# Reading raw blocks of w2's inner operands straight from the weights, and k of some chunks in one transfer

## The chip, the cores and the metric

The kernel runs on one core of a Trainium2 chip. The core has five engines that run their own queues of instructions in order: TensorE (PE: matmuls, with PEld for loading weights), VectorE (DVE), ScalarE (ACT), GpSimd (POOL) and SyncE (SP), which here issues nearly all DMA transfers. The metric is the time of one execution on the device in microseconds (us), given as the median of several runs.

## The reference

Two blocks follow each other, all in fp32. First a causal linear attention with a decay per head, over 4 batches, 8 heads, 768 positions and head size 64; then a mixture of 4 experts over the 3072 tokens (512 wide), with hidden size 1024 and 512 outputs, weighted by normalized probabilities:

```python
# attention, per block of 64 positions
intra = (qb @ kb^T * Dmask) @ vb
inter = (qb * lam_pow) @ kv_state
out   = intra + inter
kb_dec   = kb * rev_pow
kv_state = lam_block * kv_state + kb_dec^T @ vb
...
# experts, on x = the attention's output, 3072 x 512
p = domain_probs / (domain_probs.sum(-1, keepdims=True) + 1e-09)
for e in range(E):                       # E = 4
    h = np.maximum(x @ w1[e], 0.0)       # w1[e] is 512 x 1024
    out += p[:, e:e + 1] * (h @ w2[e])   # w2[e] is 1024 x 512
```

## The kernel before, in words

**Tiling.** The tokens are cut into 24 chunks of 128 and 3 groups of 8 chunks. A *unit* is one group with one expert, 12 in all, in the order (0,0) (0,1) (0,2) (0,3) (1,1) (1,2) (1,3) (1,0) (2,2) (2,3) (2,0) (2,1). Each unit has a first product (x with w1, lines 1125 to 1165) and a second one (hidden with w2). Both use Strassen-Winograd's scheme: seven products M1 to M7 of blocks, where one operand is a block of the weights (A11, A12, A22) or a sum of blocks (S1 to S4), and the other is a block or a sum of blocks (T1 to T4) of the data. The operands are: M1 uses A11, M2 A12, M3 S4, M4 A22, M5 S1, M6 S2, M7 S3. In what follows, M1, M2 and M4 are *A-type* products and M3, M5, M6 and M7 are *S-type* products.

**The nested second product.** From unit 5 on (`NEST`), each of the seven products of the second product is itself done by the scheme: in order M1, M3, M5, M7, M6, M2, M4 (`SEQ3`), each with seven inner products in the order M1, M7, M6, M4, M5, M2, M3 (`INNER`). For that, each product's weight operand is cut in four and its inner sums S1 to S4 are needed as well: seven inner operands (A11, S3, S2, A22, S1, A12, S4), each of 128 x 2 x 128 numbers, 128 KB. They are made once for each expert, stored in device memory as `w2_ops[expert, product]`, and read back for each unit.

**Making them.** `prepare_w2_ops` (line 335) gives a list of *chores*: load blocks of w2 (`block`, tile w2b, 256 KB per transfer), add or subtract them on POOL (`total`, tile w2o), and, by `ready`, call `inner_w2` (line 322), which makes the four inner sums of one product on POOL (tile ops, four operations of 128 x 256) and queues their storing. Of one product, all seven operands are stored, also those which are plain blocks of w2. The chores of the four experts are appended in the order 2, 3, 0 (before unit 0) and 1 (at unit 5). Those of experts 3, 0 and 1 are *eased*: they use another pool of tiles and end with M6, M2, then the total S4 and M3. Expert 0 is used first in unit 7, expert 1 in unit 11, which is the last (`FINAL`); there M2 is done without nesting (`PLAIN`), straight from the weights.

**Reading them.** `feed3` (line 1249) loads the operands of one product for PE into four tiles w2t (two operands each; six such tiles are there in turn). It is called some tiles ahead of their use. In unit 11 all products but the first are read as one whole tile (w2s). Line 1514 holds the inner matmuls that use the tiles, line 1207 the second products that are not nested, line 1148 the first products. `tt` (line 117) is the helper through which all additions on VectorE and POOL go, `send` (line 114) the one for nearly all transfers.

**What sets the order.** The program writes out all instructions in one pass, with a clock `now` that counts steps of PE's work. After each step `pump` (line 202) may begin the next chore. It does so only if the counts of the planner allow it: `asked` (0.27 for each transfer sent through `send`) and `moved` (by the bytes of a transfer and the length of its contiguous pieces) must be less than `FULL` = 4 ahead of `now`, and the last chore's spacing, 5 or 7 steps in the nested part, must be over. Stores wait in a queue until 8 steps after POOL's counted work. Where an operand is needed that has not been made and stored, `until` (line 226) begins chores and stores, all that is needed, without regard to these counts:

```python
def until(what):
    while what not in made:
        pump(force=True)
```

The engines then run what was written, each in its own order, as soon as what it waits for is there. Transfers on SP's queue are issued in order, so one that waits for its data holds up all behind it.

**Attention.** The 24 chunks go through a pipeline beside the products of the experts. `load` (line 155) fetches q, k and v of a chunk, `decayed` (line 657) multiplies k with the decay on POOL. The chunks from 13 on *come across* (`comes_across`, line 481): their q and k are also copied to device memory in another layout and turned on VectorE instead of PE. Their k in natural layout is still needed for the state, and is fetched by two transfers, one for each half of the heads, straight through SP and not through `send`.

Of the kernel before, what the change touches and what calls it, by code (L numbers as in the profile page):

```python
# [12 lines left out]
ALU = mybir.AluOpType  # L13
# [8 lines left out]
def kernel(  # L22
# [30 lines left out]
    nc = tc.nc  # L53

    B, H, S, D = q.shape
# [3 lines left out]
    C = P  # L59
# [32 lines left out]
    def small(name):  # L92
        return pool.tile([P, W], FP32, name=name, tag="t")
# [66 lines left out]
    def load(n, names="qkv"):  # L160

        c, b = where(n)
        for name in names:
            x = ({"k": acc_tile, "v": w2_tile} if n < CPG else {}).get(name, small)(f"{name}n")
            src = {"q": q, "k": k, "v": v}[name][b, :, c * C:(c + 1) * C, :]
            if name == "v":
                to, of = x[:].rearrange("p (h d) -> p h d", d=D), src.rearrange("h p d -> p h d")
                for h in (slice(0, 4), slice(4, 8)) if n < CPG else (slice(0, 8),):
                    send(out=to[:, h], in_=of[:, h], by=nc.scalar if n == 0 and h.start else None)
            else:  # L170
                to, of = x[:].rearrange("p (i r d) -> p i r d", r=2, d=D), src.rearrange("(r i) p d -> p i r d", r=2)
                for r in range(2):
                    by = nc.scalar if n == 0 and r == 1 else nc.sync
                    by.dma_start(out=to[:, :, r], in_=of[:, :, r])  # L174
            nat[n, name] = x[:].rearrange("p (h d) -> p h d", d=D)


# [15 lines left out]
    def store(f):  # L193
        queue.append((busy[0] + (8 if spare else 2), f))
# [31 lines left out]
# [3 lines that stand above are left out]
# [91 lines left out]


    INNER = ("M1", "M7", "M6", "M4", "M5", "M2", "M3")

    def inner_w2(e, m, blk, two):
        b = {f"A{i + 1}{j + 1}": blk[j][:, :, i * P:(i + 1) * P] for i in range(2) for j in range(2)}
        s = [x.rearrange("p c d -> p (c d)").rearrange("p (k c d) -> p k c d", k=2, c=2) for x in two("ops")]
        for name, x, y, op in S_OPS:
            b[name] = s[SLOT[name] // 2][:, SLOT[name] % 2]
            tt(nc.gpsimd, b[name], b[x], b[y], op)
        to = w2_ops[e, MS.index(m)]  # L330
        b["S3"] = s[0]
        at = (("A11", 0), ("S3", slice(1, 3)), ("A22", 3), ("S1", 4), ("A12", 5), ("S4", 6))
        store(lambda: ([send(out=to[:, x], in_=b[n]) for n, x in at], made.add(("w2", e, m))))

    def prepare_w2_ops(e, eased):
        st = {}

        def two(name):
            if eased:
                t = [small(name)[:] for _ in range(2)]  # L340
            else:
                t = stage.tile([P, 2, W], FP32, name=name, tag="st")
                t = [t[:, q] for q in range(2)]
            return [x.rearrange("p (c d) -> p c d", c=2) for x in t]

        def block(name, i, j):
            t = st[name] = two("w2b")
            for q in range(2):
                r = j * W + q * 256
                src = moe_w2[e, r:r + 256, i * DH:(i + 1) * DH]  # L350
                send(out=t[q], in_=src.rearrange("(c p) d -> p c d", p=P))

        def total(name, a, b, op):
            t = two("w2o")
            for q in range(2):
                tt(nc.gpsimd, t[q], st[a][q], st[b][q], op)
            st[name] = t

        def ready(m):
            inner_w2(e, m, st[A_OF[m]], two)  # L360

        if not eased:
            return weight_steps(block, total, ready)

        def less():
            a, b = st["A11"], st.pop("A21")
            for q in range(2):
                tt(nc.gpsimd, b[q], a[q], b[q], ALU.subtract)
            st["S3"] = b

        def drop(*names):
            for n in names:
                del st[n]

        return [
            lambda: (block("A21", 1, 0), block("A22", 1, 1)), pause(6),
            lambda: total("S1", "A21", "A22", ALU.add),
            lambda: (ready("M4"), block("A11", 0, 0), drop("A22")), pause(4),
            less, lambda: ready("M7"), lambda: (ready("M1"), drop("S3")), lambda: ready("M5"),
            lambda: (total("S2", "S1", "A11", ALU.subtract), block("A12", 0, 1)), lambda: ready("M6"),  # L380
            lambda: ready("M2"),
            lambda: total("S4", "A12", "S2", ALU.subtract), lambda: ready("M3"),
        ]

# [96 lines left out]
    def comes_across(n):  # L481
        return n >= FIRST_ACROSS
# [174 lines left out]
    def decayed(n):  # L657

        kn = nat[n, "k"]
        kd = kn if n >= CPG else small("kd")[:].rearrange("p (h d) -> p h d", d=D)  # L660
        nat[n, "kd"] = kd
        by = k_decay.rearrange("p r ac -> p ac r").unsqueeze(3).to_broadcast([P, NHP, 2, D])
        tt(nc.gpsimd, *(x.rearrange("p (ac r) d -> p ac r d", r=2) for x in (kd, kn)), by, ALU.mult)

    carried = set()

# [20 lines left out]
    def turn(n, tags):  # L687
        all_added()
        begin_state(n)
        if comes_across(n):  # L690
            turn_across(n)
            return
        if n < CPG:
            decayed(n)
        qn, kn = nat.pop((n, "q")), nat[n, "k"]
        qp = bank(tags[0], "qp")
        kp = bank(tags[1], "kp")
        for x, y in ((qp, qn), (kp, kn)):
            for ac in range(NHP):
                nc.tensor.transpose(  # L700
                    out=x[:, ac * C:(ac + 1) * C], in_=y[:, 2 * ac:2 * ac + 2].rearrange("p r d -> p (r d)"),
                    identity=ident[:],
                )
        if n >= CPG:
            decayed(n)
        del nat[n, "k"]
        qT, kT = small("qT"), small("kT")
        nc.scalar.copy(out=qT[:], in_=qp[:])
        nc.scalar.copy(out=kT[:], in_=kp[:])
        if n >= CPG:  # L710
            turned[n] = qT, kT, qT
            return
        qs = small("qs")
        scaled = lambda: scale_q(qs, qp)
        soon(n, scaled)
        turned[n] = qT, kT, qs, scaled

    def scores(n, tags):
# [19 lines left out]
        for ac in range(NHP):  # L738
            for x in range(1 if last else 2):
                for r in range(2):  # L740
                    nc.tensor.matmul(  # L741
                        out=sp[x][half[r], 256 + ac * D:256 + (ac + 1) * D], lhsT=kd[half[x], 2 * ac + r],
                        rhs=vn[half[x], 4 * r + ac], start=False, stop=True, skip_group_check=True,
                    )
        st = small("st")
# [503 lines left out]
    def feed3(e, m, k):  # L1249

        x_e = units[e][1]
        until(("w2", x_e, m))
        if e == FINAL and m != SEQ3[0]:

            if k == 0:
                t = xp.tile([P, 7, 256], FP32, name="w2s", tag="x" + SEQ[SEQ3.index(m)])
                if (e, m) == PLAIN:
                    i, j = int(A_OF[m][1]) - 1, int(A_OF[m][2]) - 1
                    src = moe_w2[x_e, j * W:(j + 1) * W, i * DH:(i + 1) * DH]
                    send(out=t[:, 0:4], in_=src.rearrange("(k p) d -> p k d", p=P))  # L1260
                    fed3[e, m, 0] = t
                    return
                send(out=t[:], in_=w2_ops[x_e, MS.index(m)].rearrange("p k c d -> p k (c d)"))
                for x in range(4):
                    fed3[e, m, x] = t[:, 2 * x:min(2 * x + 2, 7)]
            return
        t = w2pool.tile([P, 2, DH], FP32, name="w2t", tag="w2")
        n = min(2, 7 - 2 * k)
        send(
            out=t[:, 0:n], in_=w2_ops[x_e, MS.index(m), :, 2 * k:2 * k + n].rearrange("p k c d -> p k (c d)"),  # L1270
        )
        fed3[e, m, k] = t

# [218 lines left out]
    def nested_product(e, m, tags):  # L1494
# [8 lines left out]

        def inner(x, i):
            if (e, m) == END and i in ("M2", "M3"):
                turned_product(("M2", "M3").index(i), b[B_OF[i]], fed3[e, m, x // 2][:, x % 2])
                return
            t = tags[0] if i in ("M1", "M6", "M5", "M3") else tags[1]
            fresh = i in ("M1", "M7", "M2")
# [2 lines left out]
            p = banks[t]  # L1512
            for c in range(2):
                nc.tensor.matmul(  # L1514
                    out=p[:, 0:256], lhsT=fed3[e, m, x // 2][:, x % 2, c * P:(c + 1) * P],
                    rhs=b[B_OF[i]][:, c * 256:(c + 1) * 256], start=(fresh and c == 0), stop=True,
                    skip_group_check=True,
                )
# [443 lines left out]
```

## Time and profile before

| what | value |
| --- | --- |
| time, median of 3 runs | 1143.09 us (1141.39 to 1143.7) |
| time of the profiled execution | 1141.95 us |
| span from the first to the last instruction, profiled execution | 1140.2 us |
| mean granted clock of TensorE | 1.000 |
| read / written in device memory | 197.19 MB / 78.68 MB |
| transfers w2t<-w_ops of 256 KB | 129, 3.3 us from issue to landing (median) |
| transfers w2t<-w_ops of 128 KB | 43, 2.2 us |
| transfers w_ops<-ops of 256 KB / 128 KB | 28 / 56, 4.1 / 3.7 us |
| transfers w_ops<-w2b, w_ops<-w2o of 128 KB | 45 and 39, 3.9 us each |
| transfers w2b<-in_moe_w_dram of 256 KB | 56, 4.9 us |
| transfers kn<-in_k_dram of 128 KB | 47, 4.5 us |

The profile names engines PE, PEld, DVE, ACT, POOL and SP; SPq and PEq are the sequencers in front of them. L114 is line 114 of the program. A group is written as operation, tile written <- tiles read, and its count; both `w1_ops` and `w2_ops` appear as w_ops. In rows in order of time, the first number is the start, the second the duration in us from there to the end of what was merged into the row, "x6" the number of instructions, and the brackets at the end hold how long the engine stood idle before, and for what. A waiting line reads: who waited <- for whom: us in total, times, longest.

### The profile page before, as it was taken

Reading aid. Unit: us, or ns where it says so; the run is one execution under the profiler, and the core shown is the slowest. Engines: PE = TensorE matmul, PEld = TensorE weight load, DVE = VectorE, ACT = ScalarE, POOL = GpSimd, SP = SyncE. Lnnn points to the kernel's source line nnn. Section 1 sums busy time; section 2 is a strip of 40 time slices with the busy share of each in tenths; the row PEclk is TensorE's granted clock in tenths of the full one; section 3 lists DMA queues with packets and bytes.
Section 4 is the critical chain, followed back from the end, with each engine's and each line's share of the span. In section 5 each row is a group of like instructions: output and inputs, shape, how many; then the busy total and the mean of one; then the engine's idle time right before and its main releaser. Section 6 shows DMA issues by size and latency. Waiting matters only on the chain.

```text
span 1140.2 us, 22167 instructions
## 1 busy us (share of the span) xinstructions
PE 1130.8 (99%) x7991; PEld 987.7 (87%) x7991; DVE 771.7 (68%) x1472; ACT 381.1 (33%) x770; POOL 767.7 (67%) x734
## 2 busy tenths in 40 slices
PE   8999999999999999999999999999999999999998
PEld 7788888888888888888888888888888888888887
DVE  4576775588577757837655566878767576776785
ACT  4325123212312321232343442444354452342332
POOL 2747148655852984854884997995995873873885
PEclk9999999999999999999999999999999999999999
DMA  8796889899989999987867669976779757657553
GB/s 195 173 281 183 214 226 265 276 299 279 310 270 323 301 311 303 312 279 233 260 204 249 200 182 286 347 241 199 223 235 277 217 161 213 189 159 214 168 194 74
DMA packets 321436, 271.58 MB, mean 238 GB/s; under 512 B 150640, under 2 KB 256304, under 8 KB 321328
## 3 DMA queue, kind: packets, MB, share of 16 engines
q1 hardware_dynamic: 298528, 264.37, 76.1%
q10 hardware_dynamic: 22768, 5.80, 2.5%
q8 instruction: 64, 1.05, 0.4%
q14 instruction: 44, 0.36, 0.1%
q0 software_dynamic: 32, 0.00, 0.0%
HBM read 197.19 MB, written 78.68 MB: 242 GB/s over the span
## 4 chain that ended last, share of the span: by engine, by line
PE 97%; SPq 1%; DMA 1%; DVE 0%; issue 0%; ACT 0%; DVEq 0%
PE pg L1148 41%; PE pq L1514 25%; PE q L1207 21%; PE pM L1656 2%; PE pc L1656 2%; PE op L797 1%; PE sp L734 1%; PE op L815 1%; PE sp L741 1%; DMA qn<-in_q_dram 1%; SPq L114 1%; PE pM L1381 1%; PE pg L1514 1%; SPq L174 0%; PE qp L700 0%; PE kp L700 0%
## 5 line engine op out<-in xcount | busy, mean ns | idle before, releaser
L1148 PE MATMUL pg<-xs,ws_in 128*128 128x256 f32 x1960 | 470.2, 380 | 0.4 <-DVE m L117 0.4
L1148 PEld LDWEIGHTS pg<-xs,ws_in 128*128 128x128 f32 x1960 | 371.0, 190 | 53.5 <-DVE m L117 3.2
L117 DVE TENSOR_TENSOR m<-pg,m 128x512 f32<-128x512 f32 x374 | 255.4, 686 | 91.7 <-PE pg L1148 81.4
L1207 PE MATMUL q<-w2t,m 128*128 128x256 f32 x1120 | 265.6, 380 | 0.0
L1207 PEld LDWEIGHTS q<-w2t,m 128*128 128x128 f32 x1120 | 211.7, 190 | 29.3 <-issue 0.3
L117 DVE TENSOR_TENSOR sums<-pq,sums 128x256 f32<-128x256 f32 x272 | 113.1, 421 | 90.6 <-PE pq L1514 78.4
L117 POOL TENSOR_TENSOR m<-m,decay 128x512 f32<-128x512 f32 x91 | 114.5, 1271 | 82.4 <-ACT m L1165 65.4
L1514 PE MATMUL pq<-acc,w2t 128*128 128x256 f32 x688 | 169.2, 379 | 0.0
L1514 PEld LDWEIGHTS pq<-acc,w2t 128*128 128x128 f32 x688 | 130.5, 190 | 18.0
L1165 ACT ACTIVATE m<-m 128x512 f32<-128x512 f32 x99 | 62.4, 630 | 190.9 <-DVE m L117 186.7
L1225 DVE SCALAR_TENSOR_TENSOR acc<-q,gate,acc 128x256 f32<-128x256 f32 x108 | 52.0, 482 | 75.6 <-PE q L1207 74.8
L117 DVE TENSOR_TENSOR m<-m,m 128x512 f32<-128x512 f32 x108 | 96.6, 894 | 6.5 <-ACT m L1131 6.5
L1161 ACT COPY m<-pg 128x512 f32<-128x512 f32 x88 | 51.5, 586 | 121.6 <-PE pg L1148 114.2
L117 POOL TENSOR_TENSOR acc<-hT,hT 128x512 f32<-128x512 f32 x56 | 70.3, 1270 | 21.7 <-PE pq L1514 13.9
L1125 ACT COPY pg<-m 128x512 f32<-128x512 f32 x77 | 45.5, 591 | 110.2 <-DVE m L117 108.1
L117 POOL TENSOR_TENSOR acc<-hT,acc 128x512 f32<-128x512 f32 x56 | 71.2, 1272 | 7.0 <-PE pq L1514 3.2
L1514 PE MATMUL pq<-hT,w2t 128*128 128x256 f32 x288 | 70.0, 379 | 0.0
L117 POOL TENSOR_TENSOR w2o<-w2b 128x512 f32<-128x512 f32 x26 | 36.7, 1437 | 45.6 <-DMA w2b<-in_moe_w_dram 39.3
L1514 PEld LDWEIGHTS pq<-hT,w2t 128*128 128x128 f32 x288 | 54.7, 190 | 7.4
L117 POOL TENSOR_TENSOR kn<-kn,decay 128x512 f32<-128x512 f32 x16 | 19.1, 1197 | 55.9 <-PE kp L700 29.8
L1129 ACT COPY m<-pg 128x512 f32<-128x512 f32 x44 | 25.7, 585 | 91.8 <-PE pg L1148 91.8
L1514 PE MATMUL pq<-m,w2t 128*128 128x256 f32 x228 | 55.4, 379 | 0.0
(157 smaller groups left out, 1453.3 us busy)
## 6 DMA issues: line engine op xcount, KB each, us to landing
w2t<-w_ops SPq DMA_DIRECT2D x129, 256.0 KB, 3.3
ws_in<-w_ops SPq DMA_DIRECT2D x40, 512.0 KB, 4.7
ws_in<-w_ops SPq DMA_DIRECT2D x60, 256.0 KB, 4.0
ws_in<-w_ops SPq DMA_DIRECT2D x40, 384.0 KB, 4.3
w2b<-in_moe_w_dram SPq DMA_DIRECT2D x56, 256.0 KB, 4.9
w_ops<-ops SPq DMA_DIRECT2D x28, 512.0 KB, 4.7
w2t<-w_sums SPq DMA_DIRECT2D x40, 256.0 KB, 4.7
w_sums<-w2o SPq DMA_DIRECT2D x16, 512.0 KB, 5.4
```

What stands on the lines that cost most here:

```text
L114: (by or nc.sync).dma_start(out=out, in_=in_)
L117: eng.tensor_tensor(out=o, in0=a, in1=b, op=op)
L734: nc.tensor.matmul(out=sp[r][half[x], ac * BL:(ac + 1) * BL], lhsT=hc(kT)[half[r], ac, blk[x]], rhs=hc(qT)[half[r], ac, blk[x]], start=(ac ...
L1125: nc.scalar.copy(out=banks[tags[1]][:], in_=new["11"][:])
L1129: nc.scalar.copy(out=o[:], in_=p[:])
L1148: nc.tensor.matmul(out=p[:, j * 256:(j + 1) * 256], lhsT=ws[i][:, j * P:(j + 1) * P], rhs=xs[i], start=(fresh and j == 0), stop=True, skip ...
L1161: nc.scalar.copy(out=new[at][:], in_=p[:])
L1165: nc.scalar.activation(out=new[at][:], in_=new[at][:], func=AF.Relu)
L1207: nc.tensor.matmul(out=p[:, s * DH:(s + 1) * DH], lhsT=h[A_OF[m]][:, c * 256 + s * P:c * 256 + (s + 1) * P], rhs=fed2[g, e, m][uu][:, c], ...
L1225: nc.vector.scalar_tensor_tensor(out=o, in0=x, scalar=w, in1=o, op0=ALU.mult, op1=ALU.add)
L1514: nc.tensor.matmul(out=p[:, 0:256], lhsT=fed3[e, m, x // 2][:, x % 2, c * P:(c + 1) * P], rhs=b[B_OF[i]][:, c * 256:(c + 1) * 256], start= ...
L1656: nc.tensor.matmul(out=p[:, s * 256:(s + 1) * 256], lhsT=a[c][:, f:f + P], rhs=b[:, c, j * 256:(j + 1) * 256], start=(s == 0 and c == 0 an ...
```

## The change

Two things are changed.

- *Raw blocks.* Of A-type products, only the four sums are stored; the three inner operands that are plain blocks (A11, A12, A22 of the block) are not stored and are read from `moe_w2` itself by `raw_w2`, in rows of 512 bytes. The order of the seven operands in `w2_ops` becomes A11, S3, S2, S1, S4, A12, A22 (`OPS_AT`), so the four sums lie side by side, and two transfers store them. S-type products still store all seven; there A12 and A22 go in one transfer where the tile's layout allows it (`together`), since `total` now writes its result with the halves of the columns outermost. In `feed3`, a tile of an S-type product that holds two operands which are not neighbours any more is read by one transfer with a stride; a tile of an A-type product is read piece by piece. M2 of expert 1, which is used without nesting only, is not made any more.
- *k in one transfer.* For chunks that come across, k is fetched by one transfer through `send` (and so counted in `asked` and `moved`), in the order of the heads in memory. `decayed` and the matmuls that read k are given the new layout.

```diff
@@ load
                 to, of = x[:].rearrange("p (i r d) -> p i r d", r=2, d=D), src.rearrange("(r i) p d -> p i r d", r=2)
-                for r in range(2):
-                    by = nc.scalar if n == 0 and r == 1 else nc.sync
-                    by.dma_start(out=to[:, :, r], in_=of[:, :, r])
+                if comes_across(n):
+                    to = x[:].rearrange("p (r i d) -> p i r d", r=2, d=D)
+                    send(out=x[:].rearrange("p (h d) -> p h d", d=D), in_=src.rearrange("h p d -> p h d"))
+                else:
+                    for r in range(2):
+                        by = nc.scalar if n == 0 and r == 1 else nc.sync
+                        by.dma_start(out=to[:, :, r], in_=of[:, :, r])
+                nat[n, name] = to
+                continue
@@ inner_w2
+    OPS_AT = {"A11": 0, "S3": 1, "S2": 2, "S1": 3, "S4": 4, "A12": 5, "A22": 6}
+
+    def raw_w2(e, m, name):
+        (i, j), (x, y) = ((int(n[1]) - 1, int(n[2]) - 1) for n in (A_OF[m], name))
+        r, d = j * W + y * 256, i * DH + x * P
+        return moe_w2[e, r:r + 256, d:d + P].rearrange("(c p) d -> p c d", p=P)
...
         to = w2_ops[e, MS.index(m)]
-        b["S3"] = s[0]
-        at = (("A11", 0), ("S3", slice(1, 3)), ("A22", 3), ("S1", 4), ("A12", 5), ("S4", 6))
-        store(lambda: ([send(out=to[:, x], in_=b[n]) for n, x in at], made.add(("w2", e, m))))
+        pieces = [(to[:, 1 + 2 * x:3 + 2 * x], s[x]) for x in range(2)]
+        if A_OF[m][0] == "S":
+            pieces += [(to[:, 0], b["A11"])]
+            if together(blk[1]):
+                pieces += [(to[:, 5:7], blk[1].rearrange("p c i d -> p i c d"))]
+            else:
+                pieces += [(to[:, OPS_AT[n]], b[n]) for n in ("A12", "A22")]
+        store(lambda: ([send(out=x, in_=y) for x, y in pieces], made.add(("w2", e, m))))
@@ prepare_w2_ops
         def total(name, a, b, op):
-            t = two("w2o")
+            t = [x.rearrange("p (i c d) -> p c i d", c=2, i=2) for x in two("w2o")]
...
-            lambda: ready("M2"),
+            *([lambda: ready("M2")] if e != units[FINAL][1] else []),
             lambda: total("S4", "A12", "S2", ALU.subtract), lambda: ready("M3"),
@@ decayed
+        if comes_across(n):
+            kd, kn, by = (x.rearrange("p i r d -> p r i d") for x in (kd, kn, by))
+        tt(nc.gpsimd, kd, kn, by, ALU.mult)
@@ feed3
-        until(("w2", x_e, m))
+        ops, ready = w2_ops[x_e, MS.index(m)].rearrange("p k c d -> p k (c d)"), A_OF[m][0] == "S"
+        if (e, m) != PLAIN:
+            until(("w2", x_e, m))
...
-                send(out=t[:], in_=w2_ops[x_e, MS.index(m)].rearrange("p k c d -> p k (c d)"))
+                if ready:
+                    send(out=t[:], in_=ops)
+                else:
+                    send(out=t[:, 1:5], in_=ops[:, 1:5])
+                    for n in ("A11", "A22", "A12"):
+                        send(out=t[:, OPS_AT[n]].rearrange("p (c d) -> p c d", c=2), in_=raw_w2(x_e, m, n))
...
-        n = min(2, 7 - 2 * k)
-        send(
-            out=t[:, 0:n], in_=w2_ops[x_e, MS.index(m), :, 2 * k:2 * k + n].rearrange("p k c d -> p k (c d)"),
-        )
-        fed3[e, m, k] = t
+        names = [A_OF[i] for i in INNER[2 * k:2 * k + 2]]
+        fed3.update({(e, m, i): t[:, x] for x, i in enumerate(INNER[2 * k:2 * k + 2])})
+        stored = [n for n in names if ready or n[0] == "S"]
+        for n in names:
+            if n not in stored:
+                send(out=t[:, names.index(n)].rearrange("p (c d) -> p c d", c=2), in_=raw_w2(x_e, m, n))
+        x, y = OPS_AT[stored[0]], OPS_AT[stored[-1]]
+        at = names.index(stored[0])
+        send(out=t[:, at:at + len(stored)], in_=ops[:, x:y + 1:max(y - x, 1)])
```

## The prediction

> **What bounds the kernel now.** I read the page's head first (busy time, chain), then the time of PE stage by stage, then the waits of PE and of the DMA queue, and last the order of time on POOL, SP and PE around one place. The head says that TensorE is busy 99% and makes up 97% of the chain that ended last:
>
> ```profile
> span 1140.2 us, 22167 instructions
> PE 1130.8 (99%) x7991; PEld 987.7 (87%) x7991; DVE 771.7 (68%) x1472; ACT 381.1 (33%) x770; POOL 767.7 (67%) x734
> PE 97%; SPq 1%; DMA 1%; DVE 0%; issue 0%; ACT 0%; DVEq 0%
> ```
>
> The windows (length, then busy PE, PEld, DVE, ACT, POOL, then granted clock) say where PE is not busy:
>
> ```profile
> 50.00:1138.00 1088.00, 1086.39 (x6940) 951.26 (x6939) 745.87 (x1389) 360.60 (x714) 745.63 (x707) 1.00 0.79 241
> 1138.00:1140.00 2.00, 0.00 (x0) 0.00 (x0) 0.00 (x0) 0.00 (x0) 0.00 (x0) 0.78 0.24 67
> ```
>
> Of 1088 us PE is idle 1.61, and 1.16 of that follow its last row (1135.78 + 1.06 = 1136.84). So between 50 us and the last matmul PE loses 0.45 us in all, at 340 us, for VectorE (pg of line 1148). Whatever the change takes off POOL, SP or the DMA engines can win that much and no more; it can only lose by making PE wait for an operand. So the question is whether each operand is still early enough. The waits of SP say how the loads are paced: SP waits for PE to free the buffers of w2t, 3.2 us at a time, and now and then for POOL:
>
> ```profile
> SPq L114 <- PE pq L1514: 240.3, 125, 3.2
> ...
> SPq L114 <- POOL ops L117: 9.9, 9, 3.9
> ```
>
> **The change, part by part.**
>
> *k in one transfer.* 11 chunks (13 to 23) ask for k once instead of twice: 11 DMAs fewer, at about 0.4 us of SP each (the rows of single DMAs below). PE and ACT keep their order of instructions. SP has 240 us of waits in which those 4.4 us lie, so this is 0; without that cover it would be 4.4 us spread over 11 places. The decay multiply gets another stride (r outermost, runs of 64 elements in both orders); its group has 1.197 us x16 now. No row shows the new stride. Bounds: the x8 group of the same size at 1.059 and the slowest of this size, 1.437 (w2o<-w2b); 11 multiplies, -1.5 to +2.6 us, on POOL, which is idle a third of the span. 0.
>
> *Stores.* 28 products of w2's operands were stored by 6 DMAs each (168). Now 11 take 2, 13 take 4, 3 take 5, and M2 of expert 1 is not made: 22 + 52 + 15 = 89, 79 fewer. M2's four POOL operations at 0.775 us (ops<-w2b) save 3.1 us of POOL. 0, by the same cover. *Loads.* Each A-type product is read by 7 DMAs, not 4: 20 such readings, 3 more each, 60. SP's total is 79 + 11 - 60 = 30 fewer, some 12 us of its time. Raw blocks come in rows of 512 bytes, their landing no row shows: bounds 2.2 us (w2t<-w_ops of 128 KB) and 4.4 (w2t<-in_moe_w_dram of 256 KB); I take 3.3. Their use lies 7 us or more after issue in the rows of tile w2t that I followed, so 0; with no cover it would be up to 2 us for each of 60. S-type tiles 1 and 2 are read in two runs of 1 KB instead of one of 2 KB: bounds 2.2 and 4.4 again, against 3.3, 0.
>
> *The order of the chores: this is where it loses.* A chore is begun only where the planner's count of DMAs asked for and bytes moved is less than 4 us ahead. The 60 more loads and k's DMAs (outside the count before) add to it, so the chores of expert 0 slip. Setting the two built kernels' instruction lists side by side: expert 0's last product M3 (S4 total, four ops, stores) stood well ahead of its use; now its chore is still unpaid when the load for M3 is asked for. `until` then forces all that is left: S4, ops, stores, and the next expert's four w2b loads of 256 KB, in SP's queue straight ahead of the load of w2t that PE needs next. PE needs it at 763.80 (the first matmuls of M3 in unit 7). Before, POOL made the operands by 726.1, they were stored from 735.83 to 740.63 and loaded at 749.25:
>
> ```profile
> 711.77 1.27 POOL L117 TENSOR_TENSOR m<-m,decay 128x512 f32<-128x512 f32 x1 [5.81 <-ACT m L1165]
> ...
> 715.47 2.50 POOL L117 TENSOR_TENSOR w2o<-w2b,w2o 128x512 f32<-128x512 f32 x2
> ...
> 723.09 1.41 POOL L117 TENSOR_TENSOR ops<-w2o 128x256 f32<-128x256 f32 x2
> 724.58 0.72 POOL L117 TENSOR_TENSOR ops<-ops,w2o 128x256 f32<-128x256 f32 x1
> 725.38 0.73 POOL L117 TENSOR_TENSOR ops<-w2o,ops 128x256 f32<-128x256 f32 x1
> ...
> 732.47 7.42 POOL L117 TENSOR_TENSOR m<-m,decay 128x512 f32<-128x512 f32 x6
> ```
>
> ```profile
> 728.53 2.10 SPq L114 DMA_DIRECT2D w2b<-in_moe_w_dram  x4
> 730.72 0.42 SPq L114 DMA_DIRECT2D w2t<-w_ops  x1
> ...
> 735.83 1.30 SPq L114 DMA_DIRECT2D w_ops<-w2o  x1
> ...
> 749.25 4.71 SPq L114 DMA_DIRECT2D w2t<-w_ops  x3
> ```
>
> ```profile
> 763.80 1.03 PE L1514 MATMUL pq<-m,w2t 128*128 128x256 f32 x4
> ```
>
> When does POOL have M3 now? The changed kernel's POOL queue, from the multiply that starts at 711.77 (POOL had just waited 5.81 us for ACT, so nothing is carried over) to the third of M3's ops, which completes S2 and S3, holds: the ops of M1, M5, M6 and M2 at 2.97 (723.09 to 726.06), 11.9; totals S2 and S4 at 2.45, 4.9; 11 m multiplies at 1.24 (7.42/6), 13.6; 12 acc additions at 1.29 (half of the pairs at 717.92 to 723.09), 15.5; three of M3's ops, 2.2. Together 48.1: **759.9**, if nothing waits. Five of them (M1, M5, S2, M6, M2) stood ahead of 711.77 before; that is the difference. SP then issues the stores at some 0.4 each, A11's third, at 761.2. A 128 KB store lands after 3.6 us (w_ops<-w1o; 3.9 for w_ops<-w2o): 764.8. The four w2b loads (2.1 us of SP) pass in between, and only then can the w2t load go out, for it reads what the store wrote. Its landing, from the view of tile w2t between 685 and 770:
>
> ```profile
> DMA to landing us min/median/max: 2.0/4.1/8.8
> ```
>
> 764.8 + 4.0 = **768.8**, so PE waits 768.8 - 763.8 = **5.0 us**. I take near the median, with w2b's 1 MB under way, since the load at 730.72 behind four w2b loads landed at 735.77, 5.05 later. Low bound: POOL 0.7 earlier, the store at 2.2 (the shortest row of 128 KB, w2t<-w_ops), the load at 2.0, which leaves 1 to 2. High bound of this case: the store at 5.4 (the slowest row, w_sums<-w2o), the load at 5.05, which makes 8.
>
> Behind the waiting load SP holds the other tiles of M3, then ws_in and xs, each wanted later than the first and issued 0.4 to 1.2 us apart: the one wait covers them. Behind M3's ops POOL holds four acc additions, 760.7 to 765.9, wanted one by one from 764.66 (pq<-acc,w2t); the first is done at 762.0, so they add nothing.
>
> *The clock after the stall.* PE stops for 5 us. At the end of the profile it stopped at 1136.84, and the clock of 1138 to 1140 averages 0.78: t + 0.5 (2 - t) = 1.56 puts the fall at 1139.1, 2.3 us after. At the start four transposes took 1.06 us at 4.42 and 0.63 at 6.01, so full speed came some 3.4 to 4.9 us after the first matmul at 1.06. A stall past 2.3 us thus costs 0 to 4.9 us at half speed, 0 to 2.4; I take 1.5, as the wait is twice as long as the 2.3. The Trainium skill, "TensorE: Matmul & The Clock Gate", section "Part 1: The HAM clock gate", asks for a whole idle window of about 3.4 us, free-running, before the clock halves. The profile's 2.3 us disagrees with that. By the page a stall of 5.0 us would hold a whole window in (5.0 - 3.4)/3.4 = 47% of cases, and this term would be 0.47 x 2.4 = 1.1 by estimate, and the sum would be 0.4 less.
>
> *Sum.* 1141.95 (the profiled execution, 1.75 around its span of 1140.2) + 5.0 + 1.5 = 1148.4. The median 1143.09 lies 1.14 above the profiled execution; I add half, 0.6: **1149.0**.
>
> **Rivals.**
>
> (a) *The wait is covered* (0.12). If POOL is ahead of my sum or store and load land at their least, the stall is under 2 us, with no fall of the clock: 1141.95 + 0 to 2 + 0.6 = 1142.5 to 1144.5. For it: POOL idles a third of the span, and the load's minimum is 2.0. Against: by its queue POOL has no idle time left between 711.77 and 759.9.
>
> (b) *The load queues behind the 1 MB of w2b* (0.10). For it: the 8.8 us above belong to a load issued from 692.76 on, right behind two w2b loads. Then the stall is 8 to 11: 1152.9 to 1155.9.
>
> (c) *Faster* (0.03). With 79 fewer stores and 5 MB less written, SP reaches its loads earlier, and PE's small waits go: the profile has 0.45 us of them, which gives 1141.5 by the profiled execution. To pass 0.2% (1140.8) the timed runs would have to hold more such waits than the profiled one. It decides only if M3's load lands before 763.8, 5 us earlier than in my sum.
>
> The rest (0.02) is another operand late, likeliest at 340 to 370 us, where the DMA engines are busiest.
>
> **How the numbers follow.** 0.73 for the forecast, 1144.5 (stall 2, no fall of the clock) to 1152.9 (8 and 2.4). 0.2% is 2.3 us, about what a measurement tells from no change. Slower by more: above 1145.4, nearly all of the forecast and (b), 0.82. Within: (a) and the low end of the forecast, 0.15. Faster: (c), 0.03. The range 1143.5 to 1154 leaves out (c), half of (a) and half of (b), about 0.16 with the rest.
>
> **What would show it.** After: a PE wait at line 1514 for a DMA (w2t<-w_ops) of 3 to 7 us near 764, once; the S4 total on POOL past 750; stores of M3 past 759; a granted clock under 1.00 within the 6 us behind the wait; PE's busy time up by that, elsewhere unchanged. The step on POOL is wrong if M3's ops run before 750; the step on SP if the load lands within 5 us of the operands. PE waits of over 1 us elsewhere, or none, make the prediction wrong.

## The result, and the profile after

The changed kernel takes 1155.71 us (median of 5 runs, 1154.29 to 1156.32) beside 1143.7 us of the kernel before on the same chip (5 runs, 1141.39 to 1144.85): 12.0 us more, a ratio of 1.0105 with a 95% interval of 1.0091 to 1.0118. The forecast was 1149.0 with a range of 1143.5 to 1154.0. It had the sign, but half the loss, and the time lies above the range.

(In the kernel's listing above, `load` begins at line 160 and `inner_w2` at line 324, not at the lines given in the words before it.)

The profiled execution took 1154.29 us. The head of its page and its chain (the first five numbers are busy time per engine; the last line is the chain that ended last):

```profile
span 1152.5 us, 22126 instructions
PE 1136.2 (99%) x7991; PEld 990.7 (86%) x7991; DVE 768.9 (67%) x1472; ACT 381.4 (33%) x770; POOL 765.5 (66%) x730
PE 93%; SPq 3%; DMA 2%; DVE 1%; issue 0%; ACT 0%; DVEq 0%
```

The span grew by 12.3 us. PE does the same 7991 matmuls, yet is "busy" 5.4 us longer (1136.2 against 1130.8) and idle 6.9 us longer (16.3 against 9.4). Both have to be explained: waits make idle time, and the same matmuls are busy longer where the granted clock is lower, as the windows below show. The waits of PE, over the whole span (total, times, longest):

```profile
PE pq L1551 <- DMA w2t<-w_ops: 5.0, 1, 5.0
PE kp L727 <- DMA kn<-in_k_dram: 3.1, 3, 1.8
PE pg L1175 <- DVE m L117: 2.0, 1, 2.0
```

The first is the forecast wait, of exactly the forecast size. The second lies in the first 50 us, where PE is busy as long as before (44.57 us against 44.38). The third was 0.4 us before. The order of time on PE around the two waits (start, duration, in brackets the idle time before):

```profile
344.45 1.89 PE L1234 MATMUL q<-w2t,m 128*128 128x256 f32 x8
348.30 3.45 PE L1175 MATMUL pg<-xs,ws_in 128*128 128x256 f32 x8 [1.97 <-DVE m L117]
351.55 0.87 PE L1234 MATMUL q<-w2t,m 128*128 128x256 f32 x2
...
766.33 1.89 PE L1175 MATMUL pg<-xs,ws_in 128*128 128x256 f32 x8
773.18 2.04 PE L1551 MATMUL pq<-m,w2t 128*128 128x256 f32 x4 [4.96 <-DMA w2t<-w_ops]
775.02 1.91 PE L1551 MATMUL pq<-acc,w2t 128*128 128x256 f32 x4
776.73 2.90 PE L1175 MATMUL pg<-xs,ws_in 128*128 128x256 f32 x8
779.46 1.89 PE L1551 MATMUL pq<-acc,w2t 128*128 128x256 f32 x8
```

Eight matmuls take 1.89 us at full clock and 3.45 us behind the first wait; four take 1.03 us at full clock and 2.04 us behind the second. Since PE has the same order in both kernels behind the first 50 us, the time of the same matmul in both profiles gives the account. The shift is +0.3 us at 341 (340.68 to 340.99), +3.25 at the row that starts at 348.30 before and 351.55 after, +4.26 where PE last ran freely (762.07 to 766.33), +9.38 behind the long wait (763.80 to 773.18), +12.2 once the clock is back (771.57 to 783.78) and +12.46 at the last row (1135.78 to 1148.24). So, near 346, a wait of 2.0 in place of 0.4, and 1.7 of half clock; near 370, 0.8 (0.5 of it a wait that the profile shows); near 770, 5.1 of waiting and 2.8 of half clock; the rest, some 0.3 at each end.

The windows of the same profile, cut where the clock changed (length, busy PE, PEld, DVE, ACT, POOL, granted clock):

```profile
345.27:348.68 3.41, 1.44 (x7) 0.94 (x7) 1.33 (x3) 0.40 (x1) 0.57 (x1) 1.00 1.09 274
348.68:352.10 3.42, 3.42 (x10) 2.67 (x9) 2.67 (x3) 0.72 (x2) 3.38 (x3) 0.50 1.01 350
...
768.52:771.94 3.42, 0.00 (x0) 0.00 (x0) 0.12 (x1) 0.87 (x2) 3.34 (x4) 1.00 0.93 290
771.94:775.35 3.41, 2.17 (x5) 1.84 (x6) 0.09 (x1) 0.00 (x0) 3.33 (x4) 0.50 1.03 374
775.35:778.76 3.41, 3.41 (x9) 2.69 (x9) 1.96 (x4) 0.04 (x1) 2.05 (x3) 0.50 1.10 351
```

The clock is halved for whole stretches of 3.41 us, one behind the short wait and two behind the long one. PE loses half of what it is busy in them: 3.42/2 = 1.7, and (2.17 + 3.41)/2 = 2.8.

How the operands of the long wait came about, on POOL and then on SP (the changed kernel):

```profile
759.25 2.50 POOL L117 TENSOR_TENSOR w2o<-w2b,w2o 128x512 f32<-128x512 f32 x2
761.70 1.42 POOL L117 TENSOR_TENSOR ops<-w2o 128x256 f32<-128x256 f32 x2
763.20 0.73 POOL L117 TENSOR_TENSOR ops<-ops,w2o 128x256 f32<-128x256 f32 x1
```

```profile
754.36 10.72 SPq L114 DMA_DIRECT2D w_ops<-ops  x4
765.13 0.94 SPq L114 DMA_DIRECT2D w_ops<-w2o  x2
766.12 2.02 SPq L114 DMA_DIRECT2D w2b<-in_moe_w_dram  x4
768.24 1.39 SPq L114 DMA_DIRECT2D w2t<-w_ops  x3
```

S4 is made from 759.25 on, M3's third operation ends at 763.93. SP sends M2's two stores from 754.36 on, then stands on M3's until POOL is done (8.2 us), and sends A11's at 765.13; four w2b loads follow, then, with no wait between, the load of w2t at 768.24. It lands 4.8 us later, and PE goes on at 773.18. This is the chain that the prediction worked out. It leaves open why the chores were late, what made the wait near 346, and what sets the price in clock.

### The profile page after: what moved, and what is told of

Same layout as the page of the kernel before. It is cut to its first block, busy times and chain, and to the rows that moved or that the text cites. A ratio compares the mean times of both kernels' runs of the same rounds, so it can differ in the third digit from the quotient of the medians.

```text
span 1152.5 us, 22126 instructions
## 1 busy us (share of the span) xinstructions
PE 1136.2 (99%) x7991; PEld 990.7 (86%) x7991; DVE 768.9 (67%) x1472; ACT 381.4 (33%) x770; POOL 765.5 (66%) x730
## 4 chain that ended last, share of the span: by engine, by line
PE 93%; SPq 3%; DMA 2%; DVE 1%; issue 0%; ACT 0%; DVEq 0%
PE pg L1175 40%; PE pq L1551 24%; PE q L1234 20%; SPq L114 3%; PE pc L1693 2%; PE op L824 1%; PE pM L1693 1%; PE sp L761 1%; SPq L178 1%; PE sp L768 1%; PE op L842 1%; DMA w2b<-in_moe_w_dram 1%; PE pM L1418 1%; PE pg L1551 1%; DMA w2t<-w_ops 0%
## 5 line engine op out<-in xcount | busy, mean ns | idle before, releaser
L117 DVE TENSOR_TENSOR m<-m,m 128x512 f32<-128x512 f32 x108 | 92.1, 853 | 6.5 <-ACT m L1158 6.5
```

Of the source, the lines that this page charges most:

```text
L117: eng.tensor_tensor(out=o, in0=a, in1=b, op=op)
```

## The experiments

Three theories of why the chores are late were put against each other. A: the count of k's transfer in the planner alone moves the chores. B, the prediction's: the 60 more loads of the raw blocks move them as well. C: the transfers themselves are late or slow, k's single one near 346 and the raw blocks' near 768.

### Raw blocks alone

```diff
@@ load (on the changed kernel)
-                if comes_across(n):
-                    to = x[:].rearrange("p (r i d) -> p i r d", r=2, d=D)
-                    send(out=x[:].rearrange("p (h d) -> p h d", d=D), in_=src.rearrange("h p d -> p h d"))
-                else:
-                    for r in range(2):
-                        by = nc.scalar if n == 0 and r == 1 else nc.sync
-                        by.dma_start(out=to[:, :, r], in_=of[:, :, r])
+                for r in range(2):
+                    by = nc.scalar if n == 0 and r == 1 else nc.sync
+                    by.dma_start(out=to[:, :, r], in_=of[:, :, r])
@@ decayed
-        if comes_across(n):
-            kd, kn, by = (x.rearrange("p i r d -> p r i d") for x in (kd, kn, by))
```

> The raw blocks alone; k of every chunk comes in two transfers that the planner does not count, as before. Theory A (the count of k alone moves the chores, so the raw blocks are free): 1142.5 to 1144, no PE wait for w2t near 764 and the wait near 346 back to 0.4 us. Theory B (the prediction's: the 60 more loads counted also move the chores): 1147 to 1150, with M3 of expert 0 still late. Theory C (one transfer of k lands later and is what VectorE and PE wait for near 346, and the raw loads are what is slow near 764): the wait near 764 stays, about 1151.

Measured: 1143.51 us (median of 10), ratio 1.0003, interval 0.9989 to 1.0018. Neither wait is there; PE's last matmul ends at 1136.6, as before. The chores stand where they stood before, though the 60 loads are there and counted: POOL does the same operations in the same order as in the kernel before, up to 746 us, where M2 of expert 1 is left out. B and C fall for the raw blocks: 79 stores fewer and 60 loads more, together, change nothing that can be measured.

### k in one transfer, not counted

```diff
@@ load (on the changed kernel)
-                    send(out=x[:].rearrange("p (h d) -> p h d", d=D), in_=src.rearrange("h p d -> p h d"))
+                    nc.sync.dma_start(out=x[:].rearrange("p (h d) -> p h d", d=D), in_=src.rearrange("h p d -> p h d"))
```

> The changed kernel, but the one transfer of k is issued without being counted by the planner. Theory A: chores in the order of before, 1142.5 to 1144, both waits gone, k in one transfer being worth nothing. Theory B: 1147 to 1150. Theory C: the wait of 2 us near 346 and its half clock stay (about +3.7), so 1147.

Measured: 1143.39 us (median of 10), ratio 1.0, interval 0.9991 to 1.001. With all of the change's transfers in place and only the planner's count of k's left out, the whole loss is gone. PE's waits behind 50 us are down to this line:

```profile
PE pg L1175 <- DVE m L117: 1.0, 2, 0.5
```

### k in two transfers, counted

```diff
@@ load (on the changed kernel; count is the two counting statements of send alone)
-                    send(out=x[:].rearrange("p (h d) -> p h d", d=D), in_=src.rearrange("h p d -> p h d"))
+                    count(out=x[:].rearrange("p (h d) -> p h d", d=D), in_=src.rearrange("h p d -> p h d"))
+                    for r in range(2):
+                        nc.sync.dma_start(out=to[:, :, r], in_=of[:, :, r])
```

> The changed kernel, with k in two transfers as before but counted by the planner as the one transfer is. Theory A: the same order of chores as the changed kernel, so 1155 to 1157 with both waits (2 us near 346, 5 us near 773). Theory C: the wait near 346 goes, 1152. Theory B: as A.

Measured: 1157.26 us (median of 4), ratio 1.013, interval 1.0113 to 1.0147. The count without the single transfer gives the loss, all of it. Its waits of PE from 200 us on:

```profile
PE pq L1556 <- DMA w2t<-w_ops: 4.7, 1, 4.7
PE pg L1180 <- DVE m L120: 2.2, 1, 2.2
PE sp L773 <- DMA vn<-in_v_dram: 1.8, 1, 1.8
```

With the two kernels above, the square is full: counted or not decides (1155.7 and 1157.3 against 1143.5 and 1143.4), one transfer or two does not. C falls.

### The kernel before, with k's counted transfer alone

The edit is the part of the change in `load` and `decayed`, with the indexing of k that goes with it, on the kernel before:

```diff
@@ load (on the kernel before)
+                if comes_across(n):
+                    to = x[:].rearrange("p (r i d) -> p i r d", r=2, d=D)
+                    send(out=x[:].rearrange("p (h d) -> p h d", d=D), in_=src.rearrange("h p d -> p h d"))
```

> The kernel before with k in one counted transfer, and w2's operands all stored and read as before. Theory A: the chores slip as in the changed kernel and the six stores of each product come on top: M3 of expert 0 later by some 5 us of POOL and 5 us of SP, a wait of 8 to 14 us near 764 with 3 us of half clock, maybe one more near 679 for M3 of expert 3, which is forced too: 1160 to 1168. Theory B (half of the slip is the raw loads'): 1146 to 1150.

Measured: 1161.73 us (median of 4), ratio 1.0168, interval 1.0148 to 1.0188, as theory A had it. The long wait from 200 us on:

```profile
PE pq L1522 <- DMA w2t<-w_ops: 10.9, 2, 10.7
```

So the raw blocks are not merely free: once the chores are late, they take 5.7 us off the wait (10.7 to 5.0). The rows of the two profiles say where they go. Against the moment at which PE could have gone on (768.9 here, 768.1 in the changed kernel), M3's third operation ends 5.0 us later, and the load goes out 5.3 us later. Between its first m multiply and that operation, POOL has one total and four operations of one product more to do than in the changed kernel (5.4 us), so the chores have slipped further. Six stores to count for each product would do that, but no run isolates it. That the stores also stand in SP's queue in front of the load costs little (some 0.3 us): SP sends most of them while POOL still works.

The next four kernels ask which counts matter, whether the two waits belong together, and what makes the long one as long as it is.

### k counted for chunks 17 to 23 only

```diff
@@ load (on the changed kernel)
+                    if n >= CPG + 9:
+                        send(out=x[:].rearrange("p (h d) -> p h d", d=D), in_=src.rearrange("h p d -> p h d"))
+                    else:
+                        nc.sync.dma_start(out=x[:].rearrange("p (h d) -> p h d", d=D), in_=src.rearrange("h p d -> p h d"))
```

> The changed kernel, with k's transfer counted only for chunks 17 to 23 (the first of them is asked for after the loads of q and k that VectorE waited for near 346). Theory A (each wait has its own slip of chores): no wait for VectorE near 346, and the wait of 5 us near 768 stays: 1155.7 - 3 to 4 = 1151 to 1153. Rival (the waits near 346 cause the later one, or the count only harms as a sum over all eleven): near 346 as before and near 768 under 2 us, 1143 to 1146.

Measured: 1151.39 us (median of 4), ratio 1.0065, interval 1.0041 to 1.0088. The waits of PE from 200 us on hold no VectorE near 346, and the long wait stands as it was:

```profile
PE pq L1554 <- DMA w2t<-w_ops: 5.1, 1, 5.1
PE sp L771 <- issue: 0.6, 1, 0.6
```

The two waits are separate. The 7.8 us over the kernel before are the long wait with its clock (5.1 + 2.8 in the changed kernel's account). The profiled execution is the slowest of the four (1154.68) and is some 4.6 us behind the kernel before by 340, nearly all of it from the first 50 us; from 340 to 371 it falls no further behind.

### k counted for chunk 13 only

```diff
-                    if n >= CPG + 9:
+                    if n < CPG + 6:
```

> The changed kernel, with k's transfer counted for chunk 13 alone, one count of eleven. Theory A (one count is enough, since the chores then miss the stretch of 20 us near 460 in which none may begin): the wait of 5 us near 768 stays as it is, 1151 to 1157 by whether the one near 346 stays too. Rival (the slip is in proportion to the counts): a slip of one eleventh, no wait near 768, 1143 to 1145.

Measured: 1156.34 us (median of 4), ratio 1.011, interval 1.0086 to 1.0134. One count, at about 232 us, does what eleven do: the long wait is 5.0 us again, and between 336 and 371 PE falls behind by some 6 us (a wait of 1.5 us for VectorE at 346, one of 1.8 with a half clock near 370, and smaller ones). The slip does not scale with what is counted. In the program's order, chores may not begin in some stretches (`resting`: one of 15 to 20 us behind 460 and one of some 40 behind 556). By POOL's rows, the sums of expert 3's first product start at 519.6 before, and five of its products are begun ahead of the second stretch. With one count or with eleven, the chores of expert 0's w1 miss the first stretch (POOL has summed three of its products by 471 before, and starts on the first at 482 or 483 now), expert 3's first product starts at 550.8 or 549.4, and it is the only one ahead of the second stretch. That these stretches are what makes a small slip large is read from the order, not from a run of its own; that one count is enough is shown.

### More chores in the nested part

```diff
@@ pump (on the changed kernel)
-            free[0] = max(free[0], begin + max(pace * (busy[0] - was), (5 if len(chores) > 13 else 7) if spare else 1))
+            free[0] = max(free[0], begin + max(pace * (busy[0] - was), (4 if len(chores) > 13 else 7) if spare else 1))
```

> The changed kernel, with 4 steps instead of 5 between chores in the nested part as long as more than 13 are left. M3 of expert 0 is then made some 19 steps earlier. Theory A: the wait near 768 is gone with its half clock (5.0 + 2.7), the one near 346 stays: 1147 to 1149. Rival (the wait comes from SP's queue and not from the chores' order): 1154 to 1157.

Measured: 1150.48 us (median of 8, 1146.98 to 1155.19), ratio 1.0057, interval 1.0037 to 1.0078. The long wait is gone, as theory A says and its rival doesn't. The time is 1.5 us above what was expected: the profiled execution has a longer wait near 346 than the changed kernel's, and a new one at 265, although the order up to there is the same:

```profile
PE pg L1175 <- DVE m L117: 3.7, 1, 3.7
PE pg L1175 <- DMA ws_in<-w_ops: 2.2, 1, 2.2
```

Here the half clock behind the wait near 346 lasts two stretches of 3.41 us, not one. The wait near 346 thus varies with the same order on VectorE and POOL (2.0, 2.2, 2.2 and 3.7 us in the four profiled kernels that share this stretch); no run shows what makes it vary.

### M3 made ahead of M2

```diff
@@ prepare_w2_ops (on the changed kernel)
-            *([lambda: ready("M2")] if e != units[FINAL][1] else []),
             lambda: total("S4", "A12", "S2", ALU.subtract), lambda: ready("M3"),
+            *([lambda: ready("M2")] if e != units[FINAL][1] else []),
```

> The changed kernel, with M2 of each eased expert made after M3 instead of before S4 and M3. M3's ops then stand 2.97 us earlier on POOL, two stores less stand ahead of its stores on SP, and expert 1's four w2b loads no longer stand ahead of its w2t load. Theory A: the load lands some 4 us earlier, the wait is 0.5 to 1.5 us and leaves the clock alone: 1148 to 1150. Rival (the four w2b loads in front make no difference, and POOL's time alone counts): the wait is 2 us and the clock falls for 3.4 us: 1151 to 1152.

Measured: 1147.86 us (median of 10, 1143.36 to 1151.67), ratio 1.0037, interval 1.0021 to 1.0054. The long wait is not shortened but gone; PE starts M3 at 768.76 without one, as SP sends the load before M2's operands and w2b's are asked for:

```profile
761.69 1.12 SPq L114 DMA_DIRECT2D w_ops<-ops  x2
762.87 0.93 SPq L114 DMA_DIRECT2D w_ops<-w2o  x2
765.03 1.48 SPq L114 DMA_DIRECT2D w2t<-w_ops  x3
```

From the changed kernel this takes 7.7 us (12.0 over the kernel before against 4.3), which prices the long wait once more; the 4.3 us that are left are the stretch from 340 to 371, which costs 4.0 in this profile. Against the moment at which PE could have gone on (768.1 in the changed kernel, 768.76 here), M3's third operation ends 3.0 us earlier, the load goes out 3.9 us earlier, and it lands 2.6 us after its issue, where it took 4.8. So POOL's 2.97 us alone would have left 2 us of wait, as the rival said; the rest is SP, which has no w2b loads to send in front of the load, and the quicker landing. That the load lands sooner because w2b's 1 MB is not under way in front of it is likely, but no run moved that alone. The expectation of a wait of 0.5 to 1.5 us missed on the good side.

None of the eight is faster than the kernel before; the two that don't count k equal it.

## Why the prediction was right and wrong

**PE is the bound, and nothing can be won.** Right. Raw blocks alone and k uncounted give 1.0003 and 1.0 times the time before. The zeros for stores, loads and k's transfer hold as far as the engines and queues go; the raw 128 KB loads landed after 2.7 us, inside the bounds of 2.2 and 4.4.

**M3 of expert 0 is late.** Right, with luck in two terms. The times fit, allowing for the 4.26 us by which PE was late by then. M3's third operation ends at 763.93, or 759.7 (759.9 worked out); A11's store goes out at 765.13, or 760.9 (761.2); w2t's load at 768.24, or 764.0 (764.8); PE goes on at 773.18, or 768.9 (768.8). The wait is 4.96 us where 5.0 was worked out. But the prediction let the load wait 3.6 us for A11's store to land, with the w2b loads passing in between at no cost, and then land in 4.0. Measured are 3.1 and 4.9. SP did not wait for the store at all: it was busy with the four w2b loads until 768.14. Without them in front (M3 made ahead of M2), SP did wait for the store, which had landed 2.1 us after its issue. So a store priced too high, w2b loads priced at nothing and a load priced too low came out even.

**Why the chores slip.** Wrong. The step reads "the 60 more loads and k's DMAs (outside the count before) add to it, so the chores of expert 0 slip". The 60 loads, with 79 stores fewer, leave the chores where they were; the slip is k's count alone, and one count of the eleven suffices. It did not change the sum, since the late chore was read off the changed kernel's own order, but it would have pointed a repair at the wrong line.

**The clock after the stall.** Too small: 1.5 worked out, 0 to 2.4 as bounds, 2.8 measured. This term was mis-sized, and its rule was wrong. The step let the clock fall once a stall passes 2.3 us, and took the time that it stays down from the start of the kernel, up to 4.9 us, of which PE would be busy at half speed for part. But 1.97 us of waiting near 346 brought the clock down too, and it is down for whole stretches of 3.41 us, until one has passed in which PE worked most of the time: 2.17 us of work did not end it, 2.82 did (k counted for chunk 13 only). Behind 4.96 us of waiting that made two stretches in the changed kernel and lost 2.8 us. Behind the same 4.96 us with k counted for chunk 13 only it made one and lost 1.4, and behind 4.7 us (k in two transfers) one, since PE came back just as the stretch began, and lost 1.7.

**What was left out of the sum.** The larger error, and the main step that failed. "k in one transfer ... so this is 0" looked at SP's 4.4 us and at POOL's multiplies, and the chores were followed only where they make w2's operands from 685 on. But k's count moves chores from 259 us on (the sums of w1 blocks that POOL began at 259.22 before begin at 280.27 now), and what SP carries for them passes in front of the loads of q and k that come across. The changed kernel's SP:

```profile
329.62 1.43 SPq L114 DMA_DIRECT2D w_ops<-w1o  x2
331.09 2.30 SPq L114 DMA_DIRECT2D w2b<-in_moe_w_dram  x4
...
335.93 1.59 SPq L114 DMA_DIRECT2D w2b<-in_moe_w_dram  x2
337.57 2.23 SPq L114 DMA_DIRECT2D across<-in_k_dram  x3
339.84 0.61 SPq L114 DMA_DIRECT2D qx<-across  x1
343.78 0.56 SPq L114 DMA_DIRECT2D kx<-across  x1
```

The same of the kernel before:

```profile
321.38 2.60 SPq L114 DMA_DIRECT2D w2b<-in_moe_w_dram  x4
...
333.09 1.87 SPq L114 DMA_DIRECT2D across<-in_k_dram  x3
335.00 0.61 SPq L114 DMA_DIRECT2D qx<-across  x1
337.57 0.56 SPq L114 DMA_DIRECT2D kx<-across  x1
```

The loads of qx and kx go out 4.8 and 6.2 us later than before, and VectorE, which turns them in its own queue, waits (the changed kernel's VectorE in order of time):

```profile
344.24 0.71 DVE L707 STREAM_TRANSPOSE qx<-qx 128x512 f32<-128x512 f32 x1 [2.35 <-DMA qx<-across]
344.87 0.44 DVE L1252 SCALAR_TENSOR_TENSOR acc<-q,gate,acc 128x256 f32<-128x256 f32 x1
346.96 0.71 DVE L707 STREAM_TRANSPOSE kx<-kx 128x512 f32<-128x512 f32 x1 [1.65 <-DMA kx<-across]
347.60 0.65 DVE L117 TENSOR_TENSOR m<-pg,m 128x512 f32<-128x512 f32 x1
```

Behind the two transposes stands the addition that frees PE's bank, so PE waits 1.97 us and loses 1.7 more to the clock. This was the place of the one wait that PE had before (0.4 us for VectorE at 343, there for an addition just ahead of the transposes). The prediction named the place, with 0.02, as "another operand late", and said that a wait of over 1 us elsewhere would make it wrong; the sum held nothing for it. Stretch 340 to 371 costs 3.9 us in the profile (from +0.3 to +4.2) and 4.3 in the run that has only this. With it and the clock's 1.3 the forecast would have been 1154.2. Of the 1.5 us that are still missing, 0.6 are the shifts at the two ends, and 0.8 come from the median, which lies 1.4 above the profiled execution where 0.6 was added.

**Rivals.** The cover of (a) did not hold, and its "under 2 us, with no fall of the clock" is not safe either: 1.97 us brought a fall. (b), the load landing 8.8 us after its issue, did not happen; it took 4.8. (c) fell.

## What to carry to other kernels

Where a program plans its own order, list what the change adds to the planner's counts before pricing what it adds to the engines: a transfer that was free on every queue cost 12 us because it was newly counted. Read the whole order for what moved, and not only the tensors that the change names; look first at the places where the profile before already shows a wait, however small, since they have no slack. And price a wait of PE by its length and by the half clock behind it together.

## What the runs showed of the hardware

The clock's rule was not what the prediction took it for. In the changed kernel the clock fell at 348.68 and 771.94, 423.26 us apart, which is 124 stretches of 3.413 us; every stretch of half clock seen in the ten profiles is one, two or three of them long. So one grid of stretches runs through an execution, whatever PE waits for, and what PE did in one goes with the clock in the next. The 2.3 us that the prediction read at the end of the kernel before are such a case: the clock fell at 1139.1, at the end of a stretch (from 1135.72 on) with 1.11 us of work. The Trainium skill, "TensorE: Matmul & The Clock Gate", section "Part 1: The HAM clock gate", gives that length and that it runs freely, and both agree. The same section of the Trainium skill asks for a whole idle window before the clock falls, and there the runs differ: it fell behind 1.44 us of work in 3.41 above. How little work is too little is narrowed by k counted for chunk 13 only:

```profile
343.88:347.29 3.41, 1.97 (x10) 1.39 (x8) 1.35 (x3) 0.00 (x0) 2.26 (x4) 1.00 0.98 254
347.29:350.70 3.41, 3.29 (x14) 2.61 (x15) 2.23 (x5) 1.12 (x2) 0.88 (x1) 1.00 0.90 268
367.77:371.19 3.42, 1.63 (x88) 1.46 (x78) 1.07 (x3) 1.29 (x5) 0.00 (x0) 1.00 1.20 303
371.19:374.60 3.41, 3.41 (x11) 2.78 (x9) 0.69 (x1) 0.00 (x0) 2.17 (x3) 0.50 0.95 313
```

1.97 us of work (58%) kept the clock, 1.63 (48%) lost it. Behind the first 50 us of the ten profiles, every stretch at full clock with 1.78 us of work or more kept it, and every one with 1.63 or less lost it. In the first 50 us one with 1.64 kept it (the changed kernel) and one with 1.75 lost it (k counted for chunks 17 to 23), so PE's busy time is near the rule but not all of it. Up from half clock, stretches with 2.17, 2.65 and 2.71 us of work did not bring it back (the changed kernel, chunks 17 to 23, more chores), and one with 2.82 did (chunk 13 only). A wait of 1.8 us can thus cost 1.7 us more, and one of 1.5 us (the one at 346 with chunk 13 only, 1.54) nothing. Two waits of the same length can cost differently by where the stretch happens to begin: the two long waits of 4.96 us lost 2.8 and 1.4. This may be one cause of the spread of the timed runs; no run isolates that.
